# Linear attention with a gated FFN: one low part of a `w2` sum moved to GpSimd, and roundings of the attention stage moved by one tile

## The chip, the core and the metric

The kernel runs on one core of a Trainium2 chip. The metric is the device time of one execution in microseconds (us), taken over several runs. The engines are TensorE (PE in the profile; its weight loads are PEld), VectorE (DVE), ScalarE (ACT), GpSimd (POOL) and SyncE (SP), which issues the DMAs.

## What is computed

For 2048 tokens of width 576 the reference computes a linear attention with 32 heads and a feed-forward network of width 4608, both from the same normalized input, and gates the first with the second. All of it is float32.

```python
def _A_ref(x, wqkv, wo):
    q, k, v = ...                       # from x @ wqkv, 32 heads of 18
    phi = lambda t: jnp.where(t > 0, t + 1, jnp.exp(t)) + 1e-6
    pq, pk = phi(q), phi(k)
    kv = jnp.einsum("bhsd,bhse->bhde", pk, v)
    z = jnp.einsum("bhsd->bhd", pk)
    num = jnp.einsum("bhqd,bhde->bhqe", pq, kv)
    den = jnp.einsum("bhqd,bhd->bhq", pq, z)[..., None] + 1e-6
    return (num / den) @ wo             # heads put together
def _B_ref(x, w1, b1, w2, b2):
    return gelu(x @ w1 + b1) @ w2 + b2
xn = _layernorm(x)
return x + _A_ref(xn, A_wqkv, A_wo) * silu(_B_ref(xn, B_w1, B_b1, B_w2, B_b2))
```

## The kernel before, in words

**Numbers in two parts.** A matrix product in float32 is made of three products of rounded operands. Every operand is split into a high part (`hi`: ScalarE rounds it to `fp32r`) and a low part (`lo`: the source minus the high part, again rounded). `set_hi` (line 1326) is the ScalarE copy, `set_lo` (line 1329) the subtraction, which runs on the engine that it is given; nearly always that is VectorE.

**Seven products instead of eight.** The large products use a Strassen-like scheme: seven block products of sums of blocks. The sums of `w1`, of `w2` and of the activations `g` are made on GpSimd, then split. The operands of the seven `w2` products are called by the number of their product, 1 to 7; operands 5 and 6 are sums of blocks (`sum5`, `sum6`, lines 1656 to 1663).

**Stages.** First come the projections `q`, `k`, `v` and the sums over all tokens. Then comes the **attention stage** (the loop over `j` from line 1510, tiles 0 to 9 of 128 tokens, `NA` = 10). Then two halves of the feed-forward network follow, each for 1024 tokens, each with nine chunks of 512 hidden columns (`NC` = 9). The last six tiles of the attention are made beside the chunks of the second half.

**The attention stage.** In turn `j` TensorE runs `attend(j)`: 28 matmuls of tile `j` (`ps_s`, line 1287). Then it transposes tile `j+2` (`ptp`, line 1252), and ScalarE and VectorE make its high and low parts (`th`, `tl`, lines 1256 to 1258); the next use of the transposed tile waits for line 1258, the last of them. In the same turn the tiles further ahead are prepared: VectorE makes the denominators of tile `j+4` (`den`, lines 1108 to 1112) and GpSimd multiplies `q` by them into one of three buffers `vb`, `vb`, `pbuf` (`p_mult`, line 1116); GpSimd multiplies tile `j+5` by the sums of the keys (`by_sums`, `bs`, line 1101). `phi_q_hi(TO[6])` is the ScalarE part of the feature map of tile 6, and `phi_q_max(TO[6])` its maximum on VectorE (line 433); `by_sums(6)` needs it.

At the end of a turn stands `beside(j)`. It does what the feed-forward network will need. The table `RESTS` (line 1468) says in which turn a step for the **rests** runs. The rests are the last 64 rows of the inner dimension 576 = 4 x 128 + 64. `split` rounds a rest (ScalarE line 1444, VectorE line 1445) and stores it to `rq_dram` (line 543); `sums` adds pieces on VectorE (lines 534 to 538). In turn 5 `RX` is loaded back from `rq_dram` (line 1455), for the first matmuls of the feed-forward network.

**A chunk of the first half.** A chunk has 28 steps. Steps 0 to 13 are the 14 products with `w1` (`a`, `b`, `zy`, `e`, line 1576; seven for each of two column pairs). Steps 14 to 27 are the products with `w2` (`pm`, line 1738), two steps each, in the order 1, 2, 7, 4, 5, 3, 6. Product 2 goes on in the PSUM bank of product 1, 4 in that of 7, and 3 in that of 5. Each starts only when VectorE has added the bank's content to `macc` (line 1744, in chunk 0 partly line 1748). After each step the functions planned for it are called (`at_step`), so an engine's order is that of the plan. `in_order` keeps that order on VectorE, ScalarE, GpSimd and TensorE.

What matters here of the plan: `PH` (line 2028 and after) places the sums (`S`), the high and the low parts of the activations; `P0` places the sums and parts of the next chunk's first `w1` block, with the low part of `a` at step 22 (VectorE, line 1394). `W2_SUMS_HERE` (line 1921) gives for operands 6 and 5 the steps of the sum, of the high part and of the low part. The next chunk's raw `w2` block is loaded at step 22 into the one buffer `w2raw`, once its readers are done. The ninth chunk has no `P0` part, as no further `w1` block is made.

```python
W2_SUMS_HERE = {6: (4, 18, 22), 5: (5, 16, 20)}
for i, (at, hi, lo) in W2_SUMS_HERE.items():
    add(base + at, w.sum5 if i == 5 else w.sum6)
    add(base + hi, w.hi, i)
    add(base + lo, w.lo, i)
```

`gpsimd_parts` (line 1670) is a helper that was there before: it runs a two-input operation on GpSimd in two halves along the first free dimension. The sums of the activations use it.

Of the kernel before, what the change touches and what calls it, by code (L numbers as in the profile page):

```python
# [8 lines left out]
F32 = mybir.dt.float32  # L9
# [38 lines left out]
def linear_attention_gated_ffn(ctx, tc, x, xT, wqkv, wo, w1, w1e, b1, w2, b2, out):  # L48
    nc = tc.nc
    SUB, MUL, ADD = ALU.subtract, ALU.mult, ALU.add  # L50
# [42 lines left out]
    def as2(ap):  # L93
        return ap.rearrange("p (a b) -> p a b", a=2)
# [337 lines left out]
    def phi_max(key, dst, src):  # L432
        nc.vector.scalar_tensor_tensor(
            as2(dst), src, 1.000001, as2(e_of.pop(key)), op0=ADD, op1=ALU.max
        )
# [43 lines left out]
    def phi_q_hi(t):  # L479
        phi_hi(f"q{t}", as2(q_of[t]))  # L480

    def phi_q_max(t):
        phi_max(f"q{t}", q_of[t], as2(q_of[t]))
# [6 lines left out]
    class W2Round:  # L490
# [19 lines left out]
        def lo(self):  # L510
            for i, t in self.op.items():
                nc.vector.tensor_tensor(t[:, 1], self.src[i][0], t[:, 0].bitcast(F32), op=SUB)
# [547 lines left out]
    for p in range(2, NPR):  # L1060
# [4 lines left out]
    TO = [  # L1065
        2 * NPR - 3, 2 * NPR - 4, 2 * QH, 2 * QH + 1, 2 * NPR - 2, 2 * QH + 2, 2 * NPR - 1,
        2 * QH + 3, 2 * QH - 1, 2 * QH - 2,
    ]
# [30 lines left out]
    def by_sums(j):  # L1099
        e = sums_of[j] = tq.tile([P, D], F32, tag="e", name=f"bs{j}")  # L1100
        nc.gpsimd.tensor_tensor(e, q_of[TO[j]], zb[0], op=MUL)
# [19 lines left out]
    def pad(j):  # L1121
        pb = p_bufs[j % len(p_bufs)]
        nc.scalar.copy(pb[:, D:], pb[:, 512:D])
# [54 lines left out]
    def load_q(j):  # L1178
        t = TO[j]
        q_tile(t)  # L1180
        nc.sync.dma_start(q_of[t], q_dram[t])
# [110 lines left out]
    def attend(j):  # L1292
        ps = bank2(f"ps_s{j}")
        attend_mm(ps, *pT.pop(j), kw_ops)
        s_sb = stage(D, f"s{j}")
        nc.scalar.copy(as2(s_sb), ps[:, :, :HD])
        nc.sync.dma_start(s_dram[TO[j]], s_sb)
# [30 lines left out]
    def set_lo(pair, src, eng):  # L1328
        eng.tensor_tensor(pair[1], src, pair[0].bitcast(F32), op=SUB)  # L1329
# [121 lines left out]
    def load_rest(half, at, n, dst):  # L1451
# [14 lines left out]


    RESTS = {
        0: ((0, "split", 0),), 1: ((0, "sums", 0),), 2: ((0, "sums", 1), (0, "sums", 2)),
        3: ((0, "split", 1),),  # L1470
    }

    def x_part(i):
# [36 lines left out]
    for j in range(NA):  # L1510
        attend(j)
        if j + 2 < NA:
            transpose_p(j + 2)
        if j + 3 < NA:
            pad(j + 3)
        if j == 0:
            phi_q_hi(TO[6])
        if j == 1:
            phi_q_max(TO[6])
        if 0 < j < NA - 5:  # L1520
            by_sums(j + 5)
        if j + 4 < NA:
            denominators(j + 4)
            p_mult(j + 4)
        if j == 0:
            by_sums(5)
        if j == 0:
            load_q(8)
            w2_raw0.append(load_w2_raw(0))
        if j == 1:  # L1530
            load_q(9)
            load_x_pair(3, QH + 1)
            load_we(0)
        beside(j)
# [82 lines left out]
    class W2:  # L1617
# [31 lines left out]
                self.ops[i] = [t[:, 0], t[:, 1]]  # L1649
            set_hi(self.ops[i], self.src[i])  # L1650

        def lo(self, i):
            set_lo(self.ops[i], self.src[i], nc.vector)
            if self.n < NC - 1:
                keep_op(w2_dram, (self.n, i), self.tiles[i])

# [13 lines left out]
    def gpsimd_parts(dst, a, b, op):  # L1670

        for k in range(2):
            n = dst.shape[1] // 2
            cs = slice(n * k, n * k + n)
            nc.gpsimd.tensor_tensor(dst[:, cs], a[:, cs], b[:, cs], op=op)  # L1675

    class HOps:
# [6 lines left out]
        def add(self, pr, g):  # L1684
            for (par, b), t in g.items():
                self.A[pr, b, par] = t
                self.src[{(0, 0): 1, (0, 1): 2, (1, 1): 4, (1, 0): "-"}[b, par], pr] = t
# [213 lines left out]
    def plan_w1(add, w, base, T, hi, lo):  # L1901
# [7 lines left out]
        lo={"a": 0, 6: 3, "c": 4, "d": 5},  # L1909
# [4 lines left out]
        lo={"a": 22, 6: 25, "c": 26, "d": 27},  # L1914
# [3 lines left out]
    PW2 = {2: (0, 1), 1: (1, 2), 7: (3, 4), 4: (5, 6), 3: (8, 9)}  # L1918
    W2_SUMS_NEXT = {5: 23, 6: 27}
    W2_SUMS_FIRST = {5: 6, 6: 10}  # L1920
    W2_SUMS_HERE = {6: (4, 18, 22), 5: (5, 16, 20)}
    W2_NEXT = {1: 24, 2: 26, 7: 27, 4: 44, 5: 46, 3: 48, 6: 50}
    LATER_TILES = [t for t in range(2 * QH) if t not in TO]

# [9 lines left out]
    class Attention:  # L1934
# [84 lines left out]
        def store(self):  # L2019
# [14 lines left out]
        lo={  # L2034
            (1, 0): 10, (2, 0): 10, (7, 0): 11, (1, 1): 12, (2, 1): 13, (7, 1): 15, (4, 0): 16,
            (4, 1): 17, (5, 1): 18, (5, 0): 19, (6, 0): 20, (3, 0): 21, (3, 1): 22, (6, 1): 23,
        },
# [19 lines left out]
    for step in range(n_chunks):  # L2057
        half, c = divmod(step, NC)
        base = step * NS
        plain = step == n_chunks - 1  # L2060
        h = HOps(c)
# [12 lines left out]
        if half == 0:  # L2074
            plan_w1(add, w1t[2 * step + 1], base, **P1)
            add(base, w2t[step].sum7)
            for k in range(2):
                add(base + 2, w2t[step].sum4, k)
            for i, (at, lo) in PW2.items():
                add(base + at, w2t[step].hi, i)  # L2080
                add(base + lo, w2t[step].lo, i)
            if (c, 5) not in w2_dram:
                w = w2t[step]
                for i, (at, hi, lo) in W2_SUMS_HERE.items():
                    add(base + at, w.sum5 if i == 5 else w.sum6)
                    add(base + hi, w.hi, i)
                    add(base + lo, w.lo, i)
        change = step == NC - 1
        if not plain:
            for k, at in enumerate((11, 16) if change else (8, 20) if step == NC else (7, 14)):  # L2090
# [10 lines left out]
        elif not plain:  # L2101
# [8 lines left out]
            else:  # L2110
                make(W2, w2t, step + 1)

                w = w2t[step + 1]
# [118 lines left out]
```

## Time and profile before

| | |
|---|---|
| median of 3 runs | 1094.01 us (1093.94 to 1095.41) |
| the profiled execution | 1093.83 us |
| its span in the profile | 1092.0 us |
| what lies around the span | 1.83 us |
| PE busy | 1079.4 us, 99% of the span |
| DVE busy | 823.7 us, 75% |
| ACT busy | 524.8 us, 48% |
| POOL busy | 512.9 us, 47% |
| granted TensorE clock, mean | 0.999 |

Times in the timeline are from the span's start. A line of the timeline gives the start, the duration, the engine, the source line, the operation and the tiles (written from left to right as out<-in), how many like instructions were merged, and in brackets how long the engine was idle before and what released it. The chain of waits is followed back from the last instruction: at each step to what released it, or to the instruction before it on its engine. A recorded duration overlaps the next instruction's start by up to 0.1 us, so the time from start to start is the better measure of what an instruction takes from its engine.

### The profile page before, as it was taken

Reading aid. Unit: us, or ns where it says so; the run is one execution under the profiler, and the core shown is the slowest. Engines: PE = TensorE matmul, PEld = TensorE weight load, DVE = VectorE, ACT = ScalarE, POOL = GpSimd, SP = SyncE. Lnnn points to the kernel's source line nnn. Section 1 sums busy time; section 2 is a strip of 40 time slices with the busy share of each in tenths; the row PEclk is TensorE's granted clock in tenths of the full one; section 3 lists DMA queues with packets and bytes.
Section 4 is the critical chain, followed back from the end, with each engine's and each line's share of the span. In section 5 each row is a group of like instructions: output and inputs, shape, how many; then the busy total and the mean of one; then the engine's idle time right before and its main releaser. Section 6 shows DMA issues by size and latency. Waiting matters only on the chain.

```text
span 1092.0 us, 17906 instructions
## 1 busy us (share of the span) xinstructions
PE 1079.4 (99%) x6492; PEld 990.8 (91%) x6492; DVE 823.7 (75%) x1206; ACT 524.8 (48%) x872; POOL 512.9 (47%) x537
## 2 busy tenths in 40 slices
PE   8999999999999999999999999999999999999998
PEld 7999999898988989889899898998989899998988
DVE  7997853787898988989889886675847576574856
ACT  7666665635454454544545445244434434242442
POOL 3133141566586674865847644243433535252340
PEclk9999999999999999999999999999999999999999
DMA  6678634799568495685955797886767657676653
GB/s 238 195 290 225 218 127 144 237 366 376 186 228 291 174 339 178 227 291 182 330 188 216 274 391 289 295 300 214 226 202 247 202 189 244 191 227 233 212 153 139
DMA packets 91120, 258.63 MB, mean 237 GB/s; under 512 B 12182, under 2 KB 25494, under 8 KB 88728
## 3 DMA queue, kind: packets, MB, share of 16 engines
q1 hardware_dynamic: 91032, 257.49, 69.1%
q8 instruction: 51, 0.84, 0.3%
q14 instruction: 37, 0.30, 0.1%
HBM read 155.16 MB, written 101.40 MB: 235 GB/s over the span
## 4 chain that ended last, share of the span: by engine, by line
PE 89%; DVE 5%; issue 2%; ACT 2%; DMA 1%; POOL 1%; SPq 0%; DVEq 0%; POOLq 0%; ACTq 0%
PE pm L1738 31%; PE a L1576 11%; PE e L1576 10%; PE zy L1576 10%; PE b L1576 5%; PE xaall L390 4%; PE x L390 3%; PE pd L1859 2%; PE x1all L390 2%; PE psa L1287 2%; PE ps_s L1287 2%; DVE macc L1744 1%; PE ps_kva L473 1%; PE x0all L390 1%; DVE h_l L1329 1%
## 5 line engine op out<-in xcount | busy, mean ns | idle before, releaser
L1675 POOL TENSOR_TENSOR g<-g 128x256 f32<-128x256 f32 x204 | 185.3, 939 | 56.6 <-DVE h_l L1329 49.6
L1744 DVE TENSOR_TENSOR macc<-pm,macc 128x576 f32<-128x576 f32 x218 | 164.0, 752 | 45.6 <-PE pm L1738 43.8
L1326 ACT CAST h_h<-g 128x512 fp32r<-128x512 f32 x204 | 122.7, 621 | 118.6 <-PE pm L1738 117.5
L1329 DVE TENSOR_TENSOR h_l<-g,h_h 128x512 fp32r<-128x512 f32 x204 | 165.3, 817 | 2.3 <-ACT h_h L1326 2.3
L1576 PE MATMUL a<-X,wa 128*128 128x512 f32 x432 | 110.1, 390 | 0.0
L1576 PEld LDWEIGHTS a<-X,wa 128*128 128x128 f32 x432 | 79.8, 188 | 15.3
L1593 ACT COPY mid<-a 128x512 f32<-128x512 f32 x36 | 21.1, 586 | 109.6 <-PE a L1576 109.6
L1675 POOL TENSOR_TENSOR mid<-g 128x256 f32<-128x256 f32 x68 | 52.2, 788 | 45.2 <-ACT g L1584 44.1
L1596 DVE TENSOR_TENSOR mid<-b,mid 128x512 f32<-128x512 f32 x36 | 24.8, 690 | 61.6 <-PE b L1576 61.6
L1584 ACT ACTIVATE g<-b,b1c 128x512 f32<-128x512 f32 x36 | 24.8, 690 | 66.5 <-DVE b L1602 66.4
L1377 POOL TENSOR_TENSOR w1raw<-w1raw 128x256 f32<-128x256 f32 x18 | 13.3, 740 | 91.1 <-ACT h_h L1326 73.9
L1576 PE MATMUL e<-X,wc 128*128 128x512 f32 x216 | 55.6, 392 | 0.0
L1576 PE MATMUL zy<-X,wd 128*128 128x512 f32 x216 | 54.9, 389 | 0.0
L1576 PE MATMUL e<-X,wd 128*128 128x512 f32 x216 | 54.8, 389 | 0.0
L1576 PE MATMUL zy<-X,wc 128*128 128x512 f32 x216 | 54.8, 389 | 0.0
L274 POOL TENSOR_TENSOR R<-R,bc 128x640 f32<-128x640 f32 x9 | 15.8, 1776 | 71.0 <-DMA R<-xT 60.7
L1576 PEld LDWEIGHTS zy<-X,wd 128*128 128x128 f32 x216 | 40.5, 188 | 8.6
L1576 PEld LDWEIGHTS zy<-X,wc 128*128 128x128 f32 x216 | 40.5, 188 | 8.4
L1576 PEld LDWEIGHTS e<-X,wd 128*128 128x128 f32 x216 | 40.5, 188 | 8.4
L1576 PEld LDWEIGHTS e<-X,wc 128*128 128x128 f32 x216 | 40.0, 188 | 8.3 <-DVE b L1602 0.3
L1584 ACT ACTIVATE g<-e,b1c 128x512 f32<-128x512 f32 x36 | 24.8, 690 | 45.7 <-DVE e L1609 45.7
L1329 DVE TENSOR_TENSOR h_l<-mid,h_h 128x512 fp32r<-128x512 f32 x34 | 36.0, 1059 | 1.2
(1019 smaller groups left out, 3189.2 us busy)
## 6 DMA issues: line engine op xcount, KB each, us to landing
we<-we_dram SPq DMA_DIRECT2D x72, 224.0 KB
w2raw<-w SPq DMA_DIRECT2D x10, 1152.0 KB
x_dram<-X SPq DMA_DIRECT2D x6, 1792.0 KB
w1raw<-w SPq DMA_DIRECT2D x18, 512.0 KB
op_a<-wa SPq DMA_DIRECT2D x18, 512.0 KB
op_c<-wc SPq DMA_DIRECT2D x18, 512.0 KB
op_d<-wd SPq DMA_DIRECT2D x18, 512.0 KB
wc<-op_c SPq DMA_DIRECT2D x18, 512.0 KB
```

What stands on the lines that cost most here:

```text
L390: nc.tensor.matmul(dst, st, w, start=start, stop=stop, skip_group_check=True)
L1287: nc.tensor.matmul(ps[:, h, :HD], st[:, k, :], w[v][k][:, h * HD : (h + 1) * HD], start=(i == 0), stop=(i == len(seq) - 1),)
L1326: nc.scalar.copy(pair[0], src)
L1329: eng.tensor_tensor(pair[1], src, pair[0].bitcast(F32), op=SUB)
L1576: nc.tensor.matmul(ps, st, mv, start=first and n == 0, stop=n == len(seq) - 1, skip_group_check=True,)
L1584: nc.scalar.activation(g, ps, AF.Gelu_apprx_tanh, bias=b1c[:, f : f + 1])
L1593: nc.scalar.copy(m1_sb, A)
L1596: tt(u1_sb, B, m1_sb, op=ADD)
L1675: nc.gpsimd.tensor_tensor(dst[:, cs], a[:, cs], b[:, cs], op=op)
L1738: nc.tensor.matmul(ps[:, q, :HD], hs[p][st][:, cs], m[:, p, :], start=(n == 0 and i not in CHAIN), stop=(n == 5), skip_group_check=True,)
L1744: nc.vector.tensor_tensor(dst, src, dst, op=ADD)
L1859: nc.tensor.matmul(ps, st[:, cs], w_all.rearrange("p n d -> p (n d)")[:, w], start=(i == 0), stop=(i == len(seq) - 1),)
```

## The change

Three edits, none of which changes what is computed:

1. `RESTS`: each `split` and `sums` step runs one turn later (turns 1 to 4 instead of 0 to 3).
2. `phi_q_max(TO[6])` runs at the end of turn 0, behind `p_mult(4)` and `by_sums(5)` in the code, instead of in turn 1.
3. In each chunk of the first half the low part of `w2` operand 5 is made by GpSimd in two halves, at step 19, instead of by VectorE at step 20. The low part of operand 6 stays on VectorE and is made at step 20 instead of 22.

```diff
     RESTS = {
-        0: ((0, "split", 0),), 1: ((0, "sums", 0),), 2: ((0, "sums", 1), (0, "sums", 2)),
-        3: ((0, "split", 1),),
+        1: ((0, "split", 0),), 2: ((0, "sums", 0),), 3: ((0, "sums", 1), (0, "sums", 2)),
+        4: ((0, "split", 1),),
     }
...
         if j == 0:
             phi_q_hi(TO[6])
-        if j == 1:
-            phi_q_max(TO[6])
...
         if j == 0:
             by_sums(5)
+            phi_q_max(TO[6])
...
-        def lo(self, i):
-            set_lo(self.ops[i], self.src[i], nc.vector)
+        def lo(self, i, alone=True):
+            if alone:
+                set_lo(self.ops[i], self.src[i], nc.vector)
+            else:
+                h, l = self.ops[i]
+                gpsimd_parts(l, self.src[i], h.bitcast(F32), SUB)
...
-    W2_SUMS_HERE = {6: (4, 18, 22), 5: (5, 16, 20)}
+    W2_SUMS_HERE = {6: (4, 18, 20), 5: (5, 16, 19)}
...
-                    add(base + lo, w.lo, i)
+                    add(base + lo, w.lo, i, i == 6)
```

**VectorE, attention stage, turns 0 and 1.** The number in a tile's name is that of the attention tile (`den4`, `th3`); `q15` is tile 6 and `wa_rest0s0` the first rest. Before:

```order
L1112 RECIPROCAL den4_2267<-den4_2267 128x32
L1445 TENSOR_TENSOR wa_rest0s0_2278<-wa_rest0q_2194,wa_rest0s0_2278 128x512
L1257 TENSOR_TENSOR tl3_2321<-ptp3_2314,th3_2320 128x512
L1258 TENSOR_TENSOR th3_2320<-ptp3_2314,th3_2320 64x128
L433 SCALAR_TENSOR_TENSOR q15_1973<-q15_1973,eq15_2263 128x576
L1108 TENSOR_REDUCE den5_2329<-bs5_2272 128x32
L1111 TENSOR_SCALAR den5_2329<-den5_2329 128x32
L1112 RECIPROCAL den5_2329<-den5_2329 128x32
L534 SCALAR_TENSOR_TENSOR wa_rest0ef_2195<-wa_rest0ef_2195,sgn_91 128x512
L1257 TENSOR_TENSOR tl4_2380<-ptp4_2373,th4_2379 128x512
```

The same place of the changed kernel:

```order
L1112 RECIPROCAL den4_2267<-den4_2267 128x32
L433 SCALAR_TENSOR_TENSOR q15_1973<-q15_1973,eq15_2263 128x576
L1257 TENSOR_TENSOR tl3_2318<-ptp3_2311,th3_2317 128x512
L1258 TENSOR_TENSOR th3_2317<-ptp3_2311,th3_2317 64x128
L1108 TENSOR_REDUCE den5_2325<-bs5_2272 128x32
L1111 TENSOR_SCALAR den5_2325<-den5_2325 128x32
L1112 RECIPROCAL den5_2325<-den5_2325 128x32
L1445 TENSOR_TENSOR wa_rest0s0_2336<-wa_rest0q_2194,wa_rest0s0_2336 128x512
L1257 TENSOR_TENSOR tl4_2379<-ptp4_2372,th4_2378 128x512
L1258 TENSOR_TENSOR th4_2378<-ptp4_2372,th4_2378 64x128
```

The maximum has taken the place of the rest's low part ahead of tile 3, and the rest's low part stands now ahead of tile 4. In the same way the sums of lines 536 and 538 move from tile 5 to tile 6, and the second rest's low part from tile 6 to tile 7, where the low part of `wa_0` (line 1394) already stood.

**GpSimd, chunk 1, end of the activations' sums.** `g` are the activations and their sums; the row that writes `g_3450` is the sum for operand 6, the row that writes `g_3468` that for operand 3, both of the second column pair. Before:

```order
L1675 TENSOR_TENSOR mid_2762<-g_3450,g_3482 128x256 x2
L1675 TENSOR_TENSOR g_3482<-g_3482,g_3436 128x256 x2
L1675 TENSOR_TENSOR g_3450<-g_3482,g_3450 128x256 x2
L1675 TENSOR_TENSOR g_3468<-g_3468,g_3450 128x256 x2
L1377 TENSOR_TENSOR w1raw4_3281<-w1raw4_3281 128x256
```

The same place of the changed kernel:

```order
L1678 TENSOR_TENSOR mid_2762<-g_3451,g_3483 128x256 x2
L1678 TENSOR_TENSOR g_3483<-g_3483,g_3437 128x256 x2
L1678 TENSOR_TENSOR g_3451<-g_3483,g_3451 128x256 x2
L1678 TENSOR_TENSOR w2_1__3536<-w2raw1_3161,w2_1__3536 128x288 x2
L1678 TENSOR_TENSOR g_3469<-g_3469,g_3451 128x256 x2
L1377 TENSOR_TENSOR w1raw4_3282<-w1raw4_3282 128x256
```

The two halves of the low part stand ahead of the last sum.

**VectorE, chunk 1, products 7, 4, 5 and 3.** `h50_l` is the low part of activation operand 5 of the first column pair, `macc<-pm5` the addition of product 5. Before, `w2_1__3535` is the low part of operand 5 and `w2_1__3574` that of operand 6:

```order
L1744 TENSOR_TENSOR macc_2759<-pm7_3582,macc_2759 128x2x288
L1329 TENSOR_TENSOR h50_l_3599<-g_3377,h50_h_3598 128x512
L1744 TENSOR_TENSOR macc_2759<-pm7_3560,macc_2759 128x2x288
L1329 TENSOR_TENSOR w2_1__3535<-w2raw1_3160,w2_1__3535 128x576
L1329 TENSOR_TENSOR h60_l_3619<-g_3340,h60_h_3618 128x512
L1744 TENSOR_TENSOR macc_2759<-pm7_3582,macc_2759 128x2x288
L1329 TENSOR_TENSOR h30_l_3636<-g_3361,h30_h_3635 128x512
L1744 TENSOR_TENSOR macc_2759<-pm5_3641,macc_2759 128x2x288
L1329 TENSOR_TENSOR w2_1__3574<-w2raw1_3160,w2_1__3574 128x576
L1329 TENSOR_TENSOR h31_l_3661<-g_3468,h31_h_3660 128x512
L1394 TENSOR_TENSOR wa_4_3639<-w1raw4_3281,wa_4_3639 128x512
L1744 TENSOR_TENSOR macc_2759<-pm5_3667,macc_2759 128x2x288
```

The same place of the changed kernel; `w2_1__3575` is the low part of operand 6:

```order
L1747 TENSOR_TENSOR macc_2759<-pm7_3583,macc_2759 128x2x288
L1329 TENSOR_TENSOR h50_l_3604<-g_3378,h50_h_3603 128x512
L1747 TENSOR_TENSOR macc_2759<-pm7_3561,macc_2759 128x2x288
L1329 TENSOR_TENSOR w2_1__3575<-w2raw1_3161,w2_1__3575 128x576
L1329 TENSOR_TENSOR h60_l_3624<-g_3341,h60_h_3623 128x512
L1747 TENSOR_TENSOR macc_2759<-pm7_3583,macc_2759 128x2x288
L1329 TENSOR_TENSOR h30_l_3641<-g_3362,h30_h_3640 128x512
L1747 TENSOR_TENSOR macc_2759<-pm5_3646,macc_2759 128x2x288
L1329 TENSOR_TENSOR h31_l_3663<-g_3469,h31_h_3662 128x512
L1394 TENSOR_TENSOR wa_4_3644<-w1raw4_3282,wa_4_3644 128x512
L1747 TENSOR_TENSOR macc_2759<-pm5_3669,macc_2759 128x2x288
```

Operand 6 has taken the place of operand 5, and between the two additions of product 5 one instruction fewer stands.

## The prediction

> **What bounds the kernel.** I read the page first, then the chain of waits in order of time, then the timelines of the engines where the chain leaves TensorE.
>
> ```profile
> PE 1079.4 (99%) x6492; PEld 990.8 (91%) x6492; DVE 823.7 (75%) x1206; ACT 524.8 (48%) x872; POOL 512.9 (47%) x537
> ...
> PE 89%; DVE 5%; issue 2%; ACT 2%; DMA 1%; POOL 1%; SPq 0%; DVEq 0%; POOLq 0%; ACTq 0%
> ```
>
> TensorE is busy for 99% of the span, and the edits take no matmul away. Only its short waits can be won. The 5% of VectorE in the chain show that there are some. In chunk 0 the chain reads:
>
> ```profile
> 270.94 11.28 PE pm L1738 x84
> 282.25 0.76 DVE macc L1748
> 283.00 0.67 DVE w__3037 L1329
> ...
> 286.17 0.75 DVE w__3076 L1329
> 286.92 0.60 DVE h_l L1329
> 287.52 0.60 DVE wa L1394
> 288.12 0.68 DVE macc L1744
> 288.81 0.04 issue
> 288.85 5.05 PE pm L1738 x36
> 293.90 1.61 PE a L1576 x7
> ```
>
> From 282.25 to 288.81 the path runs over VectorE: it works through its queue without a pause, and product 3 for the second pair of token blocks starts at 288.85, when VectorE has added product 5 to `macc`. Both low parts of `w2` sums (`w__3037`, operand 5, and `w__3076`, operand 6) lie on that path. The products with `w2` take 293.90 - 270.94 = 22.96 us here. The other chunks tell what this costs:
>
> ```profile
> 632.90 22.60 PE pm L1738 x168
> ...
> 677.75 22.42 PE pm L1738 x168
> ```
>
> The first is the ninth chunk of the first half, which has both low parts but no `wa` behind them (line 1394): one VectorE instruction fewer, and 0.36 us less. The second is a chunk of the second half, which makes no `w2` sums: 0.54 us less. So eight chunks can each give about 0.36 us, at most 0.54.
>
> In the attention stage TensorE waits three times:
>
> ```profile
> 217.10 0.71 PE L1252 MATMUL ptp<-ident,vb 128*128 128x128 f32 x5
> 218.53 0.50 PE L1287 MATMUL ps_s<-kw_h,th 128*128 128x288 f32 x2 [0.72 <-DVE th L1258]
> ...
> 222.90 0.77 PE L1252 MATMUL ptp<-ident,pbuf 128*128 128x128 f32 x5 [0.41 <-POOL pbuf L1116]
> ...
> 228.19 0.50 PE L1287 MATMUL ps_s<-kw_h,th 128*128 128x288 f32 x2 [0.26 <-DVE th L1258]
> ...
> 231.98 0.71 PE L1252 MATMUL ptp<-ident,vb 128*128 128x128 f32 x5
> ...
> 236.25 0.71 PE L1252 MATMUL ptp<-ident,pbuf 128*128 128x128 f32 x5
> 236.71 0.51 PE L1287 MATMUL ps_s<-kw_h,th 128*128 128x288 f32 x2
> ```
>
> An undisturbed turn takes 236.25 - 231.98 = 4.27 us, of which the transpose has 236.71 - 236.25 = 0.46. Tile 3 started at 218.53, where 217.10 + 0.46 = 217.56 was possible: 0.97 lost. By the same count the transpose at 222.90 lost 222.90 - (218.53 + 3.81) = 0.56, and tile 5 at 228.19 lost 228.19 - (222.90 + 4.27 + 0.46) = 0.56. Together about 2.1 us.
>
> **The change: chunks of the first half.** VectorE loses one low part per chunk, 0.67 us from start to start (row 283.00). Operand 6 takes its place, so nothing changes for VectorE up to the first addition of product 5; from there it is 0.67 us earlier. GpSimd gets two instructions of 128x288:
>
> ```profile
> 273.88 5.13 POOL L1675 TENSOR_TENSOR g<-g 128x256 f32<-128x256 f32 x6
> ...
> 288.26 0.74 POOL L1377 TENSOR_TENSOR w1raw<-w1raw 128x256 f32<-128x256 f32 x1 [9.25 <-ACT h_h L1326]
> ```
> ```profile
> 340.44 1.43 POOL L1629 TENSOR_TENSOR w2raw<-w2raw 128x576 f32<-128x576 f32 x1 [3.69 <-DMA w2raw<-w]
> ```
> ```profile
> 277.63 0.75 DVE L1748 TENSOR_TENSOR macc<-pm,b2b 128x576 f32<-128x576 f32 x1
> 278.30 1.26 DVE L1329 TENSOR_TENSOR h_l<-g,h_h 128x512 fp32r<-128x512 f32 x1
> ...
> 280.14 0.68 DVE L1329 TENSOR_TENSOR h_l<-g,h_h 128x512 fp32r<-128x512 f32 x1
> ...
> 282.25 0.76 DVE L1748 TENSOR_TENSOR macc<-pm,b2b 128x576 f32<-128x576 f32 x1 [0.16 <-PE pm L1738]
> ```
>
> A whole 128x576 alone took 1.43 us, so the halves add some 1.5 to 1.7 us to GpSimd's run, which ended at 279.01 and then ends near 281. Before, VectorE had this low part ready only at 283.00 + 0.67 = 283.7. GpSimd's next work starts at 288.26 after 9.25 us without any, so GpSimd is in no hurry; the sum for operand 3 behind the halves still comes long before its product, whose second part starts at 288.85.
>
> What it costs is VectorE. While GpSimd runs, a low part on VectorE takes 1.26 us, as at 278.30; once GpSimd has ended, 0.68, as at 280.14. A longer run holds at least a part of one more: 0.58 us. VectorE waited 0.16 us at 282.25, which swallows that much. So VectorE comes to 282.25 later by **d = 0.58 - 0.16 = 0.42**, and to the addition at 288.12 by 0.42 - 0.67 = -0.25. Product 3 then starts 0.25 us earlier. Bounds of d: nothing (the halves fall between VectorE's two-input instructions), which gives the 0.36 of the ninth chunk; and both halves waited for from start to end, 2 x 0.8 - 0.16 = 1.44, which gives 0.67 - 1.44 = 0.77 us of loss. I take 0.42, since VectorE alternates: every second instruction there is a `macc` from PSUM, and these took 0.75 beside GpSimd (277.63) and 0.76 without it (282.25). Eight chunks: **8 x 0.25 = 2.0 us** (bounds: +2.9, at most 4.3; -6.2). The ninth chunk has no such wait: nothing.
>
> The Trainium skill ("SBUF — State Buffer", section "SBUF: two separate sides") says that a VectorE instruction with two SBUF inputs and a GpSimd one share a port pair under an exclusive lock: who starts first has it for a whole instruction. The 1.26 us agree with it. By this rule two halves can hold two VectorE instructions, and the sum would be that of the slower rival below.
>
> Operand 6 being ready some 2.8 us earlier (at 282.9 + 0.4 instead of 286.17) frees `w2raw` earlier, and so the next load on SP. GpSimd waits for it at each chunk's start (3.69 us at 340.44). What it does there is not in the chain, so I cost it at nothing. The store of operand 5 is ready earlier too and holds nothing up on SP.
>
> **The change: attention stage.**
>
> ```profile
> 211.00 0.69 DVE L433 SCALAR_TENSOR_TENSOR q<-q,eq 128x576 f32<-128x576 f32 x1
> ...
> 215.14 0.35 DVE L1112 RECIPROCAL den<-den 128x32 f32<-128x32 f32 x1
> 215.66 1.70 DVE L1445 TENSOR_TENSOR wa_rest0s<-wa_rest0q,wa_rest0s 128x512 fp32r<-128x512 f32 x1 [0.17 <-ACT wa_rest0s L1444]
> 217.38 0.69 DVE L1257 TENSOR_TENSOR tl<-ptp,th 128x512 fp32r<-128x512 f32 x1
> ...
> 218.41 0.82 DVE L433 SCALAR_TENSOR_TENSOR q<-q,eq 128x576 f32<-128x576 f32 x1
> ...
> 242.21 0.69 DVE L1257 TENSOR_TENSOR tl<-ptp,th 128x512 fp32r<-128x512 f32 x1
> ```
> ```profile
> 211.23 1.49 POOL L1116 TENSOR_TENSOR vb<-q,den 128x576 f32<-128x576 f32 x1 [1.54 <-DVE den L1112]
> ...
> 215.64 1.17 POOL L1116 TENSOR_TENSOR vb<-q,den 128x576 f32<-128x576 f32 x1 [1.54 <-DVE den L1112]
> 216.76 1.86 POOL L1101 TENSOR_TENSOR bs<-q,zb 128x576 f32<-128x576 f32 x1
> ```
>
> *Tile 3.* The rest's 1.70 us go from ahead of `tl` (217.38); the maximum comes instead, at about 215.45, and starts before GpSimd's multiplication. That pair stood at 211.00 and 211.23: 0.69 and 1.49. So the multiplication ends 0.32 later than before, at 217.13, and the transpose slips from 217.10 to 217.2; tile 3 starts at 217.7: **0.8 won**.
>
> *Tile 5's transpose* hangs on GpSimd's multiplication into `pbuf`, that on the denominators, these on `bs` (216.76). `bs` is no longer held (1.43 for 1.86: -0.43), the multiplication before it ends later (+0.32), and the maximum's 0.75 (218.41 to the next start) no longer stands in between: 0.8 earlier, the gain is kept. *Tile 5* has the sums of lines 536 and 538 no longer ahead of it: its 0.5 goes, 1.3 won.
>
> *What is late next.* In turn 4 VectorE now has both the second rest and `wa_0` ahead of tile 7's low part. The denominators of tile 9, GpSimd's last multiplication and its sums for `w1` follow one such instruction later (0.7), and with them the low part of tile 9, 242.21 + 0.7 = 242.9. Tile 3 needed 218.53 - 217.38 = 1.15 us from there, so tile 9 starts at 244.1. Before, it started at 236.71 + 4.27 + 3.81 = 244.8. **0.7 us are left.** Bounds: all 2.1 (the slack holds), or -0.5 with the loads below.
>
> ```profile
> 230.00 0.32 SPq L543 DMA_DIRECT2D rq_dram<-wa_rest0s  x1
> ...
> 236.54 5.87 SPq L1455 DMA_DIRECT2D RX<-rq_dram  x7
> ```
> ```profile
> 251.51 0.39 PE L1576 MATMUL b<-RX,we 128*128 128x512 f32 x1
> ```
>
> The second rest's store is issued some 2.7 us later, the seven loads of `RX` behind it up to as much, so the last is issued at about 244.6 for a use at 250.8. If it took as long as the store's 6.5 us until the loads could start, it would land at 251.1: 0.3 us of waiting. I expect none.
>
> **Sum.** 2.0 + 0.7 = 2.7 us; the profiled execution's 1093.83 becomes **1091.1** (span 1092.0 to 1089.3). The median of before is 1094.01, 0.2 above it.
>
> **Rivals.**
> - *Everything fits:* chunks like the ninth (2.9) and all of the attention's waits (2.1): 1093.83 - 5.0 = 1088.8. For it: the holds need a coincidence. Against: the waits in the attention move on by one tile.
> - *The wait moves in the attention:* VectorE's queue is as long as before, only in another order; nothing is won there: 1093.83 - 2.0 = 1091.8.
> - *GpSimd's hold eats the gain:* d = 0.67 is the point where nothing is left, only 0.25 above my value. Then the attention's part remains: 1093.1.
> - *Slower:* two VectorE instructions between products 7 and 4 are held in full, d = 2 x 0.58 - 0.16 = 1.00. The addition at 288.12 is then 0.33 us later than before: 8 x 0.33 = 2.6 slower, less 0.7: 1095.7. It decides from d = 0.67 on. Against it: before, no instruction was held after GpSimd's end at 279.01.
> - *The path isn't VectorE's:* the banks or loads hold TensorE anyway: 1093.8. The chain and the ninth chunk speak against it.
>
> **How the numbers follow.** Forecast 0.53 (its own range 1090 to 1092), everything fits 0.13, the wait moves 0.10, the gain eaten 0.13, slower 0.08, not VectorE's 0.03. A measurement of this kernel tells 0.2% (2.2 us) from no change, so faster means below 1091.8. From the forecast 0.47 of 0.53 are faster, all of the first rival, half of the second: 0.65. Slower 0.08, the rest 0.27. The range of 1088.7 to 1093.2 leaves out the slower case and the last one.
>
> **What would show it.** Right: the `pm` stretch of the eight chunks at about 22.7, no VectorE stretch in the chain between products 4 and 3; the wait at 218.53 gone. Wrong: the low parts of the activations at 1.26 twice more per chunk; `pm` at 22.96 or above; a wait of the first products on `RX`. The most likely error is the order in which GpSimd and VectorE meet, which the trace of before doesn't show.

## The result, and the profile after

The changed kernel takes 1088.26 us (median; 1087.33 to 1088.66), the kernel before 1093.97 us (1093.09 to 1095.41) beside it. The ratio is 0.9945 with a 95% interval of 0.9928 to 0.9963: 5.7 us faster, where 2.7 were forecast. The profiled execution of the changed kernel took 1088.02 us, with a span of 1086.1.

The page of the changed kernel, the two lines that answer to those shown of before (busy time of each engine; the chain's shares by engine):

```profile
PE 1075.6 (99%) x6492; PEld 990.6 (91%) x6492; DVE 819.6 (75%) x1197; ACT 524.4 (48%) x872; POOL 535.2 (49%) x555
...
PE 94%; ACT 2%; DMA 1%; DVE 1%; issue 1%; POOL 1%; SPq 0%; POOLq 0%; ACTq 0%; DVEq 0%
```

VectorE's share of the chain went from 5% to 1%. GpSimd is busy 22 us longer, for nine low parts of 2.5 us, and the chain does not notice. The chain in order of time, for chunk 0, the ninth chunk of the first half and the first chunk of the second half:

```profile
269.92 22.37 PE pm L1741 x168
292.30 1.61 PE a L1575 x7
...
626.88 22.37 PE pm L1741 x168
671.50 22.42 PE pm L1741 x168
```

The stretch from 282.25 to 288.81 on VectorE is gone. TensorE runs the products with `w2` without leaving the chain, and all nine chunks take 22.37 us, where before eight took 22.96 and the ninth 22.60. Now the stages: busy time of each engine from the start of GpSimd's multiplication into `pbuf` for tile 2 to the first product with `w1`, and from there to the end of the first half (length first, then busy us and instructions of TensorE, its weight loads, VectorE, ScalarE, GpSimd; last the granted clock, the DMA engines' busy share and GB/s). The kernel before:

```profile
206.75:248.68 41.93, 40.54 (x306) 39.50 (x305) 30.22 (x51) 19.35 (x37) 26.37 (x20) 1.00 0.95 346
248.68:655.50 406.82, 406.21 (x2395) 367.70 (x2395) 360.30 (x473) 204.50 (x351) 264.93 (x257) 1.00 0.72 258
```

The changed kernel:

```profile
206.40:247.66 41.26, 40.68 (x306) 39.47 (x305) 29.27 (x51) 19.28 (x37) 26.82 (x20) 1.00 0.97 351
247.66:649.25 401.59, 401.59 (x2395) 366.89 (x2395) 357.91 (x464) 204.43 (x351) 286.24 (x275) 1.00 0.72 261
```

The attention stage gave 0.67 us, the first half 406.82 - 401.59 = 5.23. What lies before gave 0.35 and what lies behind took 0.35 back, where nothing was changed. In the first half TensorE is now busy for the whole stretch.

The 5.23 us come in three parts. From the start of one chunk's products with `w2` to the next it is 44.62 us after; before, it was 45.20 (406.55 - 361.35, and the same within 0.01 for five others), 45.41 once and 45.34 once. So 8 x 0.58 = 4.64, plus 0.21 + 0.14 = 0.35 in one place (the section on e7 tells which), plus 22.60 - 22.37 = 0.23 in the ninth chunk: 5.22.

Why is it 0.58 and not 0.25? VectorE's timeline in chunk 0 of the changed kernel (start, duration, instruction):

```profile
273.82 1.02 DVE L1329 TENSOR_TENSOR h_l<-mid,h_h 128x512 fp32r<-128x512 f32 x1
...
275.43 1.25 DVE L1329 TENSOR_TENSOR h_l<-g,h_h 128x512 fp32r<-128x512 f32 x1
...
277.27 0.68 DVE L1329 TENSOR_TENSOR h_l<-g,h_h 128x512 fp32r<-128x512 f32 x1
...
278.61 1.26 DVE L1329 TENSOR_TENSOR h_l<-g,h_h 128x512 fp32r<-128x512 f32 x1
...
280.46 0.68 DVE L1329 TENSOR_TENSOR h_l<-g,h_h 128x512 fp32r<-128x512 f32 x1
281.13 0.76 DVE L1751 TENSOR_TENSOR macc<-pm,b2b 128x576 f32<-128x576 f32 x1
```

And GpSimd's:

```profile
272.85 3.28 POOL L1678 TENSOR_TENSOR g<-g 128x256 f32<-128x256 f32 x4
276.09 2.52 POOL L1678 TENSOR_TENSOR w__3037<-w2raw,w__3037 128x288 fp32r<-128x288 f32 x2
278.58 1.89 POOL L1678 TENSOR_TENSOR g<-g 128x256 f32<-128x256 f32 x2
...
289.68 1.42 POOL L1628 TENSOR_TENSOR w2raw<-w2raw 128x576 f32<-128x576 f32 x1
```

Three low parts are held (1.02, 1.25, 1.26), as many as before, and the one at 277.27, in the middle of GpSimd's halves, takes 0.68. The halves hold nothing. It is GpSimd that waits: they take 1.26 us each, where a 128x288 alone should take about 0.77 (an estimate between 0.70, the pitch of the 128x256, and 1.43 for a 128x576). VectorE starts the first addition of product 4, the row at 281.13, at 281.13 - 269.92 = 11.21 us after the products' start; before it was 282.25 - 270.94 = 11.31. So it comes there not 0.42 later but 0.10 earlier (the section on e6 tells why), and the whole 0.67 us of the removed instruction counts, up to what TensorE itself needs.

In the last row GpSimd starts its sum of `w2raw` at once. Before, it waited 3.3 to 4.2 us for that load in each of the eight chunks; now it waits in four of them, 1.25 us at most.

### The profile page after: what moved, and what is told of

Same layout as the page of the kernel before. It is cut to its first block, busy times and chain, and to the rows that moved or that the text cites. A ratio compares the mean times of both kernels' runs of the same rounds, so it can differ in the third digit from the quotient of the medians.

```text
span 1086.1 us, 17916 instructions
## 1 busy us (share of the span) xinstructions
PE 1075.6 (99%) x6492; PEld 990.6 (91%) x6492; DVE 819.6 (75%) x1197; ACT 524.4 (48%) x872; POOL 535.2 (49%) x555
## 4 chain that ended last, share of the span: by engine, by line
PE 94%; ACT 2%; DMA 1%; DVE 1%; issue 1%; POOL 1%; SPq 0%; POOLq 0%; ACTq 0%; DVEq 0%
PE pm L1741 35%; PE a L1575 11%; PE zy L1575 11%; PE e L1575 11%; PE b L1575 5%; PE xaall L390 4%; PE x L390 3%; PE pd L1862 2%; PE x1all L390 2%; PE psa L1287 2%; PE ps_s L1287 1%; PE ps_kva L473 1%; PE x0all L390 1%; PE xakv L390 1%; DMA s_dram<-s 1%
## 5 line engine op out<-in xcount | busy, mean ns | idle before, releaser
L1994 POOL TENSOR_TENSOR qa<-qa,dena 128x576 f32<-128x576 f32 x6 | 7.0, 1168 | 62.5 <-issue 56.6
```

## The experiments

The theory to be tested, **turns**: VectorE alternates a two-input low part and a `macc` that reads PSUM, 1.27 us from one low part to the next when nothing holds it. GpSimd gets one piece in beside the `macc`. If that piece is short, GpSimd asks again just before VectorE does and its second piece holds VectorE by 0.58; if it is 288 columns long, VectorE asks first and is not held. No trace shows the moment at which an engine asks; it is counted from the starts and lengths of the rows. The main rival, **length**: what counts is how long GpSimd's run is.

### e1_chunks and e2_attention: each part alone

e1 leaves the attention stage as before, e2 the chunks:

```diff
-        1: ((0, "split", 0),), 2: ((0, "sums", 0),), 3: ((0, "sums", 1), (0, "sums", 2)),
-        4: ((0, "split", 1),),
+        0: ((0, "split", 0),), 1: ((0, "sums", 0),), 2: ((0, "sums", 1), (0, "sums", 2)),
+        3: ((0, "split", 1),),
```

> Only the chunks' edit: the low part of operand 5 on GpSimd in two halves, operand 6 at step 20; the attention stage as before. Theory 'turns': GpSimd and VectorE take turns, and an instruction is held only if the other engine asked first; with halves of 128x288 VectorE is held no more often than before, so each chunk's products with w2 come to 22.37 us as in the changed kernel, the first half is 5.2 us shorter, and the time is about 5.2 us below the kernel before. Rival 'length' (my forecast's step): a longer run of GpSimd holds one more VectorE instruction by 0.58 us, and the chunks' gain beyond 2.0 us came from the shifted start of the first half; then the products stay near 22.7 us here and the gain is about 2 us.

> Only the edits of the attention stage. Both theories: the attention stage is 0.7 us shorter (the stretch from tile 2 to the first product with w1), the products with w2 of the first half stay at 22.96 us, and the time is 0.5 to 1 us below the kernel before. If the chunks' gain came from the earlier start, the products would fall to 22.4 us here and the gain would be several us.

e1: 1089.15 us, ratio 0.9951 (0.9936 to 0.9966), products 22.37 us per chunk, attention stage 41.92. e2: 1093.23 us, ratio 0.9991 (0.9981 to 1.0001); its products stand in the chain as before. Beside 1094.16 for the kernel before that is 5.0 and 0.9 us, together 5.9 for the 5.7 of both edits: within the noise the two parts add up, and the chunks carry nearly all. By its times alone e2 can't be told from the kernel before (the interval reaches 1); its profile shows the gain. But e2's attention stage is shorter than that of the changed kernel, whose code there is the same:

```profile
206.26:246.72 40.46, 40.18 (x306) 39.43 (x305) 28.39 (x51) 19.39 (x37) 26.67 (x20) 1.00 1.00 371
```

1.47 us less than before, where I expected 0.7. The section on e11 takes that up.

### e3_behind_sum: the halves behind GpSimd's last sum

```diff
-    W2_SUMS_HERE = {6: (4, 18, 20), 5: (5, 16, 19)}
+    W2_SUMS_HERE = {6: (4, 18, 20), 5: (5, 16, 20)}
```

> As the changed kernel, but GpSimd makes the two halves behind its last sum (step 20) instead of ahead of it (step 19). Theory 'turns': the low part of activation operand 4, second column pair, is held as before the change (1.26 us), those after it are not, since each half of 128x288 lets VectorE ask first; three held instructions per chunk as before the change, products with w2 at 22.4 to 22.55 us, time within 1.6 us above the changed kernel. Rival 'length': the run of GpSimd is as long as in the changed kernel and one more instruction is held, products near 22.7 us.

1088.94 us, ratio 0.9948 (0.9934 to 0.9963), products 22.45 to 22.47 us. GpSimd's two halves now run from 278.13 to 280.66. VectorE beside them:

```profile
277.46 1.25 DVE L1329 TENSOR_TENSOR h_l<-g,h_h 128x512 fp32r<-128x512 f32 x1
...
279.31 0.68 DVE L1329 TENSOR_TENSOR h_l<-g,h_h 128x512 fp32r<-128x512 f32 x1
...
281.40 0.76 DVE L1751 TENSOR_TENSOR macc<-pm,b2b 128x576 f32<-128x576 f32 x1 [0.15 <-PE pm L1741]
```

The low part at 279.31 lies wholly within the halves and takes 0.68. "Length" expected 22.7. At this place too, halves of 288 hold nothing.

### e4_256_320 and e5_whole: other pieces

```diff
-                gpsimd_parts(l, self.src[i], h.bitcast(F32), SUB)
+                for cs in (slice(0, 256), slice(256, D)):
+                    nc.gpsimd.tensor_tensor(
+                        flat(l)[:, cs], flat(self.src[i])[:, cs], flat(h.bitcast(F32))[:, cs], op=SUB
+                    )
```

e5 has `set_lo(self.ops[i], self.src[i], nc.gpsimd)` there, one instruction of 128x576.

> As the changed kernel, but the low part of operand 5 is cut into 256 and 320 columns instead of 288 and 288: the same work for GpSimd, two instructions as well. Theory 'turns': behind an instruction of 256 columns GpSimd asks 0.03 us ahead of VectorE, so the low part of activation operand 4 is held by the piece of 320 (about 1.4 us instead of 0.68) and the next by the sum behind it (1.26 us): four held instead of three, the products with w2 at 22.7 to 22.9 us, the first half some 3 to 4.5 us longer than in the changed kernel. Rival 'length': GpSimd's time is the same, so the products stay at 22.37 us and the time at that of the changed kernel.

> After, but operand 5's low part on GpSimd as one 128x576 instruction in place of two 128x288 ones. Theory (turns: what counts is whether GpSimd asks for its next instruction before VectorE asks for its next two-input one, 1.27 us after the last): the whole one is taken in VectorE's pause and lasts past that moment, so it holds one VectorE low part by about 0.6 us, and the sum behind it holds the next one by 0.58. Four held per chunk as in the run cut 256 + 320, products 22.7 to 22.9 us per chunk, 1090.3 to 1092 us. Rival (only the total length of GpSimd's run counts, and it is 0.1 us shorter than with two halves): as the changed kernel, 1088.3, products 22.37.

e4: 1091.20 us, ratio 0.9974 (0.9963 to 0.9985), against 1089.15 and 1088.94 for e1 and e3 on the same chip. The chain, and VectorE's low parts:

```profile
269.03 22.78 PE pm L1745 x168
```
```profile
274.53 1.25 DVE L1329 TENSOR_TENSOR h_l<-g,h_h 128x512 fp32r<-128x512 f32 x1
...
276.37 1.40 DVE L1329 TENSOR_TENSOR h_l<-g,h_h 128x512 fp32r<-128x512 f32 x1
...
278.37 1.25 DVE L1329 TENSOR_TENSOR h_l<-g,h_h 128x512 fp32r<-128x512 f32 x1
```

With 32 columns moved from the first piece to the second, a fourth low part is held (the one of `mid`, 1.02 at 272.93, is the first). e5: 1090.63 us, ratio 0.9964 (0.9951 to 0.9977), and its GpSimd run is even shorter than with two halves:

```profile
269.79 22.63 PE pm L1741 x168
```
```profile
275.30 1.25 DVE L1329 TENSOR_TENSOR h_l<-g,h_h 128x512 fp32r<-128x512 f32 x1
...
277.14 1.26 DVE L1329 TENSOR_TENSOR h_l<-g,h_h 128x512 fp32r<-128x512 f32 x1
...
278.99 1.26 DVE L1329 TENSOR_TENSOR h_l<-g,h_h 128x512 fp32r<-128x512 f32 x1
```

Four held again, and in the other chunks the products take 22.65 to 22.66 us. "Length" gave 1088.3 for both and falls. e5 is the kernel that the prediction described: one more low part held, 22.63 where it said about 22.7, 1090.6 us where it said 1091.1.

### e6_scalar: VectorE's relief alone

```diff
-                gpsimd_parts(l, self.src[i], h.bitcast(F32), SUB)
+                nc.scalar.copy(l, self.src[i])
```

> After, but operand 5's low part is only a ScalarE copy of the sum: the subtraction is left out, so neither VectorE nor GpSimd works for it. It shows what VectorE's relief alone is worth. Theory (turns): the sums hold three VectorE low parts per chunk as in the kernel before, and the relief of 0.67 us is all there is: products 22.37 to 22.55 us per chunk, 1088.0 to 1089.5 us, no better than the changed kernel, in which GpSimd's halves cost VectorE nothing. Rival (the prediction: the halves hold VectorE by about half of what they relieve it of): the products are below the changed kernel's 22.37 by 0.2 us or more, or the time is below 1086.7.

1089.31 us, ratio 0.9951 (0.9938 to 0.9965). With no GpSimd work for the low part at all the products take

```profile
269.36 22.47 PE pm L1741 x168
```

and three low parts are held (1.02, 1.25, 1.27). So the relief alone is worth 22.96 - 22.47 = 0.49 us per chunk, and the halves on GpSimd cost nothing beside it. The changed kernel is even 0.10 lower. In e3, in e6 and in the kernel before, VectorE waits 0.15 to 0.16 us for TensorE at the first addition of product 4; in the changed kernel it does not. Product 4 (operand `w__2868`) goes on in the bank of product 7, so its start hangs on the first addition of product 7. VectorE's row of that addition and TensorE's first row of product 4, in the kernel before:

```profile
279.48 0.74 DVE L1748 TENSOR_TENSOR macc<-pm,b2b 128x576 f32<-128x576 f32 x1
```
```profile
280.37 0.50 PE L1738 MATMUL pm<-w__2868,h_h 128*128 128x288 f32 x2
```

In the changed kernel:

```profile
277.94 0.76 DVE L1751 TENSOR_TENSOR macc<-pm,b2b 128x576 f32<-128x576 f32 x1
```
```profile
279.33 0.43 PE L1741 MATMUL pm<-w__2868,h_h 128*128 128x288 f32 x2
```

Before, the third held low part (278.30) stands ahead of this addition, which ends at 280.22, just before product 4 starts, and the two matmuls take 0.50 us for 0.43. In e3 and e6 they take 0.50 and 0.51, with the third hold at the same place. In the changed kernel and in e1 the low part there is the free one, the third hold comes behind the addition, and product 4 loses nothing. So the halves ahead of the last sum do not take a hold away, but move one to where it costs less. This is read from the rows; no run moves that addition alone.

### e7_six_late: the same relief by another way

```diff
-    W2_SUMS_HERE = {6: (4, 18, 22), 5: (5, 16, 20)}
+    W2_SUMS_HERE = {6: (4, 18, 23), 5: (5, 16, 20)}
```

This is the kernel before with operand 6's low part behind the second addition of product 5.

> The kernel before, with one edit: operand 6's low part stays on VectorE, but behind the second addition of product 5 and not ahead of it (step 23 for 22). GpSimd's instructions are those of before; operand 6 is ready later than before, and so is the next load into its buffer. Theory (VectorE's queue ahead of that addition sets the product after it, and 0.67 us less there is nearly all of the gain): products 22.4 to 22.6 us per chunk, 3 to 4.5 us faster than before, 1089.5 to 1091. Rival (the gain of the change came from the earlier load of the next sums, which GpSimd then no longer waits for): products 22.9 or more, 1093.5 to 1095.

1096.94 us, ratio 1.0024 (1.0014 to 1.0034): 2.7 us slower than before. Both expectations missed on the time. The first chunk's products are what was expected; in the eight others they take 22.67 to 22.70:

```profile
271.36 22.50 PE pm L1738 x168
```

But the next load into `w2raw` is issued at 289.41, 18.05 us after the products' start (before: 287.40, 16.46 after it; the changed kernel: 283.00, 13.08 after it), and that costs more than the relief gave: over the first half the products become 2.4 us shorter, the stretches between them 5.2 us longer. GpSimd, VectorE and TensorE of e7 behind the first chunk's products, from their own timelines:

```profile
296.07 1.44 POOL L1629 TENSOR_TENSOR w2raw<-w2raw 128x576 f32<-128x576 f32 x1 [4.27 <-DMA w2raw<-w]
```
```profile
296.64 1.42 DVE L1394 TENSOR_TENSOR wa<-w1raw,wa 128x512 fp32r<-128x512 f32 x1 [1.39 <-ACT wa L1388]
```
```profile
313.15 1.66 PE L1576 MATMUL e<-X,wc 128*128 128x512 f32 x6 [0.23 <-DVE b L1602]
```

GpSimd's sum starts 1.2 us later after these products than before and meets the low part `wa`, which takes 1.42 for 0.69. VectorE's addition `b` comes late, and TensorE waits for it: 0.22 to 0.65 us in seven of the eight chunks, 3.0 us together. But the meeting with `wa` is only one way to it: in the three chunks with the longest waits (0.63 to 0.65) the load lands so late that GpSimd's sum starts behind `wa`, which then takes 0.69; there later low parts are held longer (`wc` 1.96 us for 1.23 before, in the second chunk). What costs is the late sum. The kernel before shows the same once, at its fourth chunk (GpSimd, then VectorE):

```profile
431.38 1.44 POOL L1629 TENSOR_TENSOR w2raw<-w2raw 128x576 f32<-128x576 f32 x1 [4.24 <-DMA w2raw<-w]
```
```profile
432.28 1.08 DVE L1394 TENSOR_TENSOR wa<-w1raw,wa 128x512 fp32r<-128x512 f32 x1 [1.39 <-ACT wa L1388]
```

There the load landed later than in the other chunks, and the products behind it started 0.21 us later than in the other chunks and took 0.14 longer: the 0.35 us from above. In the changed kernel the load is issued 3.4 us earlier in the chunk, and the sum never meets `wa`. e2 and e9 issue the load as late as the kernel before, and both lose at this same chunk too. That the 0.35 come from this late sum is read from the traces; no run moves the load alone.

### e9_sums_288 and e10_sums_224: GpSimd's sums cut otherwise

The kernel before, with the sums for the activations cut into 288 + 224 columns (e9) or 224 + 288 (e10):

```diff
-            n = dst.shape[1] // 2
-            cs = slice(n * k, n * k + n)
+            cs = slice(0, 288) if k == 0 else slice(288, 512)
```

> The kernel before; only GpSimd's sums are cut into 288 and 224 columns in place of 256 and 256. No work moves. Theory (turns: a VectorE low part is held only if GpSimd asks for its next instruction less than 1.27 us after the low part's start; GpSimd gets its turn 0.54 us after that start, and a piece of 256 columns takes 0.70 us, one of 288 some 0.77, one of 224 some 0.62): behind the first held low part (the one of mid, about 1.02 us) comes one of 0.68 beside the 288 piece, then one of about 1.25 beside 224 + 288. So two low parts per chunk are held in place of three, and VectorE waits some 0.7 us at the first addition of product 5 for TensorE in place of 0.16; the time does not move, because that wait swallows it: 1093 to 1095.5 us, products 22.96 us. Rival (what counts is how long GpSimd runs): three held low parts as before.

> As the run cut 288 + 224, with the two pieces the other way round: 224 columns, then 288. Theory (turns): the 224 piece ends its 0.62 us before VectorE asks again, so each 288 piece behind it holds a low part: three held per chunk (about 1.02, 1.25 and 1.25 us), as in the kernel before; time 1093 to 1095.5 us. Rival (total length): the same as with 288 + 224, whatever that shows.

One execution each: 1093.07 and 1093.43 us, beside 1093.52 to 1096.26 for the kernel before: no difference can be told. (The wait of 0.16 us that the expectation for e9 puts at product 5 is that at the first addition of product 4.) VectorE's low parts in chunk 0 of e9:

```profile
274.67 0.69 DVE L1329 TENSOR_TENSOR h_l<-mid,h_h 128x512 fp32r<-128x512 f32 x1
...
276.03 1.19 DVE L1329 TENSOR_TENSOR h_l<-g,h_h 128x512 fp32r<-128x512 f32 x1
...
277.80 1.26 DVE L1329 TENSOR_TENSOR h_l<-g,h_h 128x512 fp32r<-128x512 f32 x1
```

and of e10:

```profile
274.56 1.02 DVE L1329 TENSOR_TENSOR h_l<-mid,h_h 128x512 fp32r<-128x512 f32 x1
...
276.16 1.25 DVE L1329 TENSOR_TENSOR h_l<-g,h_h 128x512 fp32r<-128x512 f32 x1
...
278.00 1.26 DVE L1329 TENSOR_TENSOR h_l<-g,h_h 128x512 fp32r<-128x512 f32 x1
```

Two held and three held, as "turns" counted; the same columns in another order give another count, so the length of GpSimd's run is not what decides. But in e9 the unheld one is the first, not the second, the wait at product 4 is 0.15 and not 0.7, and the products take 22.87 us and not 22.96. GpSimd's run started 2.00 us after the products' start there (1.55 before), so it met VectorE at another point. With that start the rule gives the rows as they are, but that is said afterwards. e9 speaks for the rule only half.

### e11_after, e8_spread and e12_spread: the attention stage again

e8 and e12 are one kernel: the changed one, with the third sum of the first rest and the first rounding pair of `w1` a turn later.

```diff
-        1: ((0, "split", 0),), 2: ((0, "sums", 0),), 3: ((0, "sums", 1), (0, "sums", 2)),
-        4: ((0, "split", 1),),
+        1: ((0, "split", 0),), 2: ((0, "sums", 0),), 3: ((0, "sums", 1),),
+        4: ((0, "sums", 2), (0, "split", 1)),
...
-        if j == 4:
+        if j == 5:
             w1t[0].hi("a"), w1t[0].lo("a")
-        if j == 5:
```

> After, but the third sum of the first rest is made one turn later (turn 4 for 3), and the first rounding pair of w1 one turn later too (turn 5 for 4). Theory: in the changed kernel the waits at tiles 6 and 7 (0.5 and 0.25 us) are VectorE instructions of line 538 and of the w1 rounding that stand ahead of the low part that TensorE waits for; spread out, both waits go and no new one comes up before the first products with w1: attention stage 40.6 us for 41.26, 1087.4 to 1087.9 for the whole. Rival (the wait moves on by one tile again, as it did in the change): attention stage 41.1 to 41.4 with the wait at tile 8 or 9, time as the changed kernel, 1088.3.

> The changed kernel itself, once more, beside the next run. Theory for the attention stage: its gain depends on whether GpSimd's instruction of line 1101 meets VectorE's sum of line 534 (1.9 us in the first profile of the changed kernel, 0.67 where they do not meet), so a second profile shows the stage at 40.5 or 41.3 us, and the chunks at 22.37 us as in the first. Time 1087.5 to 1089.

> The kernel of the run spread out once more, on the same chip as the changed kernel. Theory: its order keeps the waits at tiles 6 and 7 away in every execution, attention stage 40.5 us, and it is 0.3 to 0.8 us below the changed kernel, about as much as the measurement tells. Rival: those waits come and go from execution to execution in both orders, and the two medians differ by less than 0.3 us.

e8: 1087.55 us, ratio 0.9937 (0.9924 to 0.9949). On one chip e11, the changed kernel itself, took 1087.91 (ratio 0.9941, 0.9929 to 0.9954) and e12 1087.54 (0.9935, 0.9921 to 0.9948). The stage took 40.47 us in e8 as in e12. But the second profile of the changed kernel shows it without the waits as well:

```profile
206.62:247.10 40.48, 39.94 (x304) 39.15 (x303) 28.38 (x51) 19.38 (x37) 26.66 (x20) 1.00 0.99 366
```

The first profile of the changed kernel has this on GpSimd and on VectorE:

```profile
222.80 1.43 POOL L1101 TENSOR_TENSOR bs<-q,zb 128x576 f32<-128x576 f32 x1 [1.28 <-DMA q<-q_dram]
```
```profile
222.83 1.94 DVE L534 SCALAR_TENSOR_TENSOR wa_rest0ef<-wa_rest0ef,sgn 128x512 f32<-128x512 f32 x1
```

The second has:

```profile
221.71 1.42 POOL L1101 TENSOR_TENSOR bs<-q,zb 128x576 f32<-128x576 f32 x1
```
```profile
223.47 0.67 DVE L534 SCALAR_TENSOR_TENSOR wa_rest0ef<-wa_rest0ef,sgn 128x512 f32<-128x512 f32 x1
```

In the first, a load of `q` landed late, GpSimd's `bs` started 0.03 us ahead of VectorE's sum and held it, 1.94 us for 0.67. The sum of line 536 behind it started at 227.65, where e2, whose stage begins 0.14 earlier, has it at 226.66: 0.85 us late, and TensorE waited at tiles 6 and 7. e2, e4 and e6 have no such meeting and show 40.46 to 40.49 us too; in e3 GpSimd waits 0.89 us for the load, line 534 takes 1.55 us, and the stage 40.87. In e5 GpSimd waits 0.60 us for it, `bs` holds VectorE's line 1111 ahead of line 534 (1.25 us for the 0.59 of e2), and the stage takes 41.07. So the stage's gain is about 1.45 us, and 0.67 to 1.06 where this load is late. The other order of e8 does not keep the late load away: in e8's own profile GpSimd waits 0.46 us for it, and line 1111 takes 1.09 us. But TensorE does not wait at tiles 6 and 7, and the stage takes 40.47 all the same; whether that order bears a later load too is open. Its 0.4 us below the changed kernel are less than the intervals tell apart. Of e12's rival one half holds, that the waits come and go in the changed order; the medians differ by 0.37 us, which decides neither way. No version here is shown to beat the changed kernel.

## Why the prediction was wrong

*What bounds the kernel:* right. VectorE's queue ahead of product 3 set the chain in the eight chunks; taking 0.67 us from it moved the products by 0.49 with nothing put on GpSimd for it (e6).

*The chunks, 2.0 us:* wrong, 5.2 measured. The step that failed is **"A longer run holds at least a part of one more: 0.58 us."** The halves held no low part; d was -0.10 and not +0.42, so a chunk gave 0.58 and not 0.25. I took the rows at 278.30 and 280.14 for "held while GpSimd runs, free once it has ended". The runs show that a low part beside a running GpSimd can be free (279.31 in e3, 277.27 in the changed kernel), and that what decides is where GpSimd's pieces end, so their length and order: 288 + 288 three held, 256 + 320 and 576 four. For the count of held parts this is shown by e4 and e5, which came out as forecast; the order of asking behind it is inferred. The lower bound of d, "the halves fall between VectorE's two-input instructions", is nearly what happened, and I chose the value away from it. The rows could not tell me: before, GpSimd has only pieces of 256 at this place. But I took the hold of a 256 piece over to a 288 one, and did not ask what the other length does to the order in which the two engines ask.

*The 0.36 us for d at nothing:* too low as well. I took it from the ninth chunk of the kernel before and so capped the chunks' gain at 2.9 us. The relief alone gives 0.49 us per chunk (e6), and 0.09 more come from product 4's start, which the prediction did not have.

*The ninth chunk, nothing:* 0.23. Before, TensorE lost 0.07, 0.05 and 0.11 us there at the starts of products 4, 5 and 3 (by the starts of its matmuls); after, none of these.

*The second half's 22.42 as the limit:* 22.37 measured, so a chunk gave 0.58 for a limit of 0.54. That chunk was no floor: it loses some 0.05 us itself, at the start of product 4.

*The earlier load of `w2raw`, cost at nothing:* about 0.35 us, once in eight chunks. "What it does there is not in the chain" was right for chunk 0, where I looked, and not for the fourth, where the load landed later. e7 shows the price when the load is late in every chunk: slower than before, in spite of the relief.

*The attention stage, 0.7 us:* 0.67 in the first profile, and right only by chance. The give-back was forecast at tile 9, by a low part at 242.9. GpSimd's last multiplication did come 1.1 us later, at 237.08 for 235.98, but VectorE's rows of the changed kernel behind it are:

```profile
241.15 0.74 DVE L1394 TENSOR_TENSOR wc<-w1raw,wc 128x512 fp32r<-128x512 f32 x1 [0.41 <-ACT wc L1388]
242.28 0.69 DVE L1257 TENSOR_TENSOR tl<-ptp,th 128x512 fp32r<-128x512 f32 x1 [0.40 <-ACT th L1256]
```

Tile 9's low part (242.28) waited 0.40 us for ScalarE, not for VectorE's queue, and came 0.07 later, not 0.7. `wc` ahead of it took 0.74 us; that it took 1.91 before is no sign of the old order, for in e1, e7, e9 and e10, which have that order, it took 0.74 too. TensorE did not wait at tile 9 in any run. What the first profile lost, it lost at tiles 6 and 7, by the late load of `q`. Without that the stage gives 1.45: the 2.1 of the three waits, less mainly what is still lost ahead of tile 5's transpose (0.49 in e2: 216.68 to 221.44, where an undisturbed turn takes 4.27).

*The loads of `RX`, no wait:* right; the second store was issued at 232.98 for 230.00, but the loads behind it from 235.50, not later than before (236.54), and no product waited.

*The rivals:* "everything fits", 1088.8, is where the time came out, though its parts were 2.9 and 2.1 and the measured ones 5.2 and 0.7 to 1.5. "Slower" needed two more held low parts. The Trainium skill's rule ("SBUF — State Buffer", section "SBUF: two separate sides"), by which a two-input VectorE instruction and a GpSimd one exclude each other, agrees with the held low parts shown here (1.02 to 1.40 us for 0.68). That two halves could hold two VectorE instructions, as I drew from it, is what the changed kernel does not show: there it is GpSimd that waits, 1.26 us for an estimated 0.77.

## What to carry to other kernels

Where two engines shut each other out, do not price work moved from one to the other by its length: lay both queues out and ask, at each end, who asks next. Here 32 columns, some 0.07 us of GpSimd's time (an estimate, 0.77 less 0.70), decided over a hold of 0.7 us, in every round of the loop. Before a load is called harmless, look at its landing in all rounds, not in the first one.

## What the hardware showed that I had not expected

- 32 columns in one GpSimd instruction (256 for 288 in the first of two pieces) were worth 22.78 - 22.37 = 0.41 us per chunk, by one more held low part.
- One piece of 128x576 on GpSimd, 1.89 us, disturbed VectorE more than two of 128x288 with 2.52 us together: four held low parts and three.
- The same code showed its attention stage at 41.26 us in one execution and at 40.48 in another; in the first a load landed 1.28 us too late for GpSimd, whose instruction then started 0.03 us ahead of one of VectorE's and held it.
